# Another order for the front of an adaLN, H3 and SwiGLU kernel: its operations, buffers and loads, and which of two engines makes some additions

## The chip, the cores and the metric

One core of a Trainium2 chip runs the whole program. The time is device microseconds of one execution; three executions of the kernel before gave 583.09, 584.99 and 586.24 us, median 584.99.

The core has four compute engines with an instruction stream each: TensorE (PE in the profile, with its weight loads as PEld), VectorE (DVE), ScalarE (ACT) and GpSimd (POOL). SyncE (SP) issues the transfers between HBM and the on-chip memory SBUF. Every engine takes its instructions strictly in the order in which the program lists them for it, and waits on semaphores for what others have to deliver.

## The reference

All tensors are float32; 2048 tokens, 512 channels, 1792 hidden units.

```python
def _A_ref(q, k, v, shift_k, ssm_k, ssm_D):
    k_shift = sum over t < 4 of k[s - 3 + t] * shift_k[:, 3 - t]   # causal, per channel
    kv = k_shift * v
    y = causal convolution of kv with ssm_k (2048 taps, per channel, by FFT)
    return q * (y + kv * ssm_D)

def _B_ref(x, w_gate, w_up, w_down):
    return (_silu(x @ w_gate) * (x @ w_up)) @ w_down

x = A_q
mod = (_silu(c) @ w_mod).reshape(c.shape[0], 6, 1, -1)
sa, ca, ga, sb, cb, gb = (mod[:, 0], mod[:, 1], mod[:, 2], mod[:, 3], mod[:, 4], mod[:, 5])
h = _layernorm(x, axis=-1) * (1 + ca) + sa
x = x + ga * _A_ref(h, A_k, A_v, A_shift_k, A_ssm_k, A_ssm_D)
h = _layernorm(x, axis=-1) * (1 + cb) + sb
x = x + gb * _B_ref(h, B_w_gate, B_w_up, B_w_down)
return x
```

(`_A_ref` is abridged here to what it computes; the rest is the reference's own text.)

## The kernel before, in words

The program has two parts. The **front** computes everything up to the normalised input of the feed-forward block; the **feed-forward part** behind it is a steady stream of matmuls (tiles `a`, `b`, `c`, `d`, `g`, `dn`, `dq` in the profile).

The front treats the 512 channels as four blocks of 128, numbered 0 to 3, and the 2048 tokens as four tiles of 512, also 0 to 3. For one channel block it

- loads k, v and the long filter (`load_k`, `load_v`, `load_ssm`; tiles `kt`, `vt`, `ss`; 1 MiB each, some in halves or quarters), and four quarters of a transform table (`load_e`, tile `er`);
- forms the short convolution in tile `u`: `tap0` is a product by one column, `tap` a product and addition on VectorE over the whole block, and `tap2` the same split into a product on ScalarE (tile `tap`) and an addition on GpSimd;
- multiplies by v in four quarters (`times_v`, in place in `vt`), on VectorE or GpSimd;
- adds the skip weight to the first row of the filter (`skip`, one row of 128 numbers in `ss`);
- transposes the product (`x_turn`, TensorE, tile `kvt`, copied by ScalarE), and takes the first transform stage of product and filter (`x_first`, `kx_first`, `k_first`, `xk_first`: TensorE into tile `s`, copied by ScalarE to `X`, `K`, `kt` or `xk`);
- swaps rows and columns in 32x32 squares, either on VectorE (`swap_x`, STREAM_TRANSPOSE, four pieces of 128x1024 for a block) or on TensorE (`k_turn`, `xk_turn`);
- for each of eight halves of blocks `n`: takes the second stage (`x2`, tile `px`, copied by ScalarE to `xs`), sums two of its parts (`x_sum`, tile `xs` from two `xs`), multiplies with the filter's spectrum (`prod`, three VectorE products `xs<-pk,xs`), and transforms back (`inv`, tile `iv`, copied by ScalarE to `X`);
- sends the block's result to HBM and back in another layout (`put`, `get`; block 2's filter spectrum makes such a trip too, `put_k`, `get_k`), except for block 3, which VectorE transposes a second time;
- takes the last stage for a token tile (`y_pe`, tile `y`, with the inverse tables `ei` from `load_einv`, `load_einv2`).

Beside it, token tile by token tile, q is loaded (`load_x`, tile `x`), its row statistics are taken (`do_stats`, `do_aggr`; tiles `bnq`, `mva`, `rsa`), the normalised rows are formed by ScalarE (`gate_n`, tile `s`), and the modulation is multiplied in and added (`gate_m`, `gate_a`, two halves each, `s<-s,bcs`). The modulation comes from the loads of `w_mod` (`mod_load`, tile `wm`), a matmul group (`mod_rows`, tile `pb`), and a trip through HBM that spreads its rows (`mod_out`, `mod_in`, tile `bcs`). Then `y_gate` multiplies y by `s`, `add_c` adds the result to `x` with statistics of the new rows (`bnb`), `do_norm2a` closes those statistics (`mvb`, `rsb`), and `norm2b`, `norm_t`, `norm_s`, `op_hi` and `op_lo` make the first operands of the feed-forward part: normalised rows `n`, transposed `nt`, modulated `hraw`, and a pair of a rounded and a remaining part, `op`. `gu_pe` (tile `g`) is its first matmul group.

What sets the order: there is no scheduler at run time. The whole front is one list of 516 calls from line 1121 on, written in the order that is wanted, and each engine gets its instructions in that order. A function marked `@parts` is called several times, and each call does its next part: usually first the matmuls, then the copy out of PSUM. So the position of a call sets when an engine may take the work, and also what stands behind it in the same engine's queue. SP's transfers are issued in the list's order too, and a transfer that has to wait (for a buffer that is still read, or for the transfer that had the same completion semaphore) holds up all behind it.

Which buffer an operation gets is written out as well. `HOMES` (line 32) holds, for each kind of buffer, one digit per allocation in the list's order: `e8` the 8 KiB tiles per partition (k, v, u, filters, x), `b16` the 16 KiB ones (spectra, modulation weights), `r4` and `k2` smaller ones, `xs` the sums, `ps` the PSUM banks. An operation that gets a buffer waits until its earlier user's readers are done.

The engine of some additions is an argument of the call, with a default: `times_v`, `skip` and `op_lo` go to VectorE unless `pool` is given; `x_sum`, `gate_m` and `gate_a` go to GpSimd unless `dve` is given.

Of the kernel before, what the change touches and what calls it, by code (L numbers as in the profile page):

```python
# [33 lines left out]
        "1045324542111032544"  # L34
    ),
    "e8": (
        "630215745627041562756263424634623634642623634"
    ),
    "r4": (
        "4021342012243012403124023130432143213242304130243102413204123401243012340123240104010401"  # L40
    ),
    "k2": (
        "110212021020102010201020102010201201201201201201200112"
    ),
    "xs": (
        "10101010"
    ),
# [31 lines left out]
def adaln_h3_swiglu(ctx, tc, q, kT, vT, shk, ssm, dskip, wgu, wdn, c, wmod, e_fwd, e_inv, w_c, out, out_t):  # L79
# [1053 lines left out]
    tap(0, 3, 0)  # L1133
    tap0(0, act, 1)
    tap(0, 1, 1)
    k_first(0, 3)
    k_first(0, 2)
    k_first(0, 3)
    load_ssm(2)
    load_v(0, 1)  # L1140
    load_e(1)
    kx_first(2, 2)
    load_v(0, 2)
    tap(0, 2, 1)
# [36 lines left out]
    k_turn(0, 1)
    load_v(1)
    times_v(1, 0, pool)
    load_c()
    x_first(0, 0)
    x_first(0, 2)
    times_v(1, 1, pool)
    x_first(0, 1)
    load_ssm(1)
    swap_x(2)  # L1190
    times_v(1, 2, pool)
    k_turn(0, 0)
    load_k(2)
    load_wc()
    k_turn(0, 1)
    k_turn(0, 2)
    k_turn(0, 3)
    tap0(2, dve)
    k_turn(0, 2)
    k_turn(0, 3)  # L1200
    times_v(1, 3, pool)
    swap_x(3)
    k_first(1, 1)
    kx_first(2, 0)
# [24 lines left out]
    x_sum(1)
    tap(2, 2)  # L1230
    do_stats(2, 0)
    k_first(1, 0)
    x_first(1, 0)
    x_first(1, 1)
    x_first(1, 2)
    x_first(1, 2)
    x_first(1, 3)
    x_first(1, 1)
    k_turn(1, 2)
    k_turn(1, 2)  # L1240
    prod(1, 1)
    x_first(1, 3)
    prod(1, 0)
    tap2(2, 3, 0)
    swap_x(0)
    tap2(2, 3, 0)
    swap_x(1)
    x2(0, 2)
    prod(1, 2)
    x2(0, 2)  # L1250
    load_k(3)
    prod(1, 1)
    do_stats(3, 1)
    prod(1, 0)
    prod(1, 2)
    x2(0, 1)
    x2(0, 1)
    tap2(2, 3, 1)
    prod(0, 1)
    prod(0, 0)  # L1260
    tap2(2, 3, 1)
    times_v(2, 0, pool)
    silu_c()
    x_sum(0, dve)
    times_v(2, 2, pool)
    prod(0, 1)
# [36 lines left out]
    silu_c()
    skip(3, pool)
    tap2(3, 3, 1)
    do_aggr(3)
    do_aggr(3)
    xk_first(2, 1)
    load_x(0)
    xk_first(2, 1)  # L1310
    xk_first(2, 2)
    tap2(3, 2, 0)
    xk_first(2, 2)
    xk_first(2, 3)
# [12 lines left out]
    do_stats(2, 2)
    tap2(3, 2, 0)
    do_aggr(2)
    do_aggr(2)  # L1330
    xk_turn(2, 2)
    load_x(1)
    swap_x(6)
    tap2(3, 3, 0)
    xk_turn(2, 1)
    xk_turn(2, 1)
    x2(3, 2)
    x2(3, 2)
    load_v(3)
    x2(3, 1)  # L1340
    x2(3, 1)
    swap_x(4)
    times_v(3, 0, pool)
    x2(2, 1)
    x2(2, 1)
    do_aggr(2)
    prod(3, 0)
    times_v(3, 1, pool)
    x_sum(3, dve)
    prod(3, 0)  # L1350
    prod(3, 1)
    x2(2, 2)
    prod(3, 1)
    prod(3, 2)
    prod(3, 2)
    do_aggr(3)
    x2(2, 2)
    do_stats(0, 1)
    mod_out()
    put(0)  # L1360
    xk_turn(2, 3)
    xk_turn(2, 3)
    do_aggr(0)
    do_stats(1, 3)
    gate_n(2, 0)
    gate_n(3, 1)
    x_turn(3, 0)
    x_turn(3, 0)
    times_v(3, 3)
    inv(3)  # L1370
    gate_n(2, 1)
    prod(2, 1)
    x_sum(2, dve)
    times_v(3, 2, pool)
    x2(5, 1)
    inv(3)
    prod(2, 0)
    inv(3)
    do_aggr(0)
    prod(2, 1)  # L1380
# [442 lines left out]
```

## Time and profile before

| | |
|---|---|
| three executions | 583.09, 584.99, 586.24 us; median 584.99 |
| the profiled execution | 586.58 us, of which the span is 584.8 |
| TensorE's granted clock over the span | 0.997 |
| HBM read and written | 74.66 MB and 38.29 MB, 193 GB/s over the span |

The profile is of one execution. Times in it are microseconds from the span's start. In a row of single instructions the columns are start, duration, engine, line of the kernel, operation, tile written and tiles read, shape and count, and in brackets the idle time of the engine before it with what ended it. All instructions carry line 63, that of the helper that records them, so they are told apart by their tiles. In a row of a stretch, the columns are its bounds and width, then the busy time of each engine with the number of instructions, the clock granted to TensorE, the busy share of the 16 DMA engines, and GB/s. A row of a wait has who waited for whom, microseconds in total, times, and the longest. A row of a group has the busy time and the mean nanoseconds of one, then the idle time before them and what ended it.

### The profile page before, as it was taken

What the parts mean: (1) busy time and instruction counts of PE and PEld (TensorE: products, weight loads), DVE (VectorE), ACT (ScalarE), POOL (GpSimd) and SP (SyncE); (2) the same over time, 40 slices, a digit from 0 to 9 for tenths busy, and PEclk for the clock granted to TensorE, in tenths of its full rate; (3) what the DMA queues carried; (4) which work ended last, traced back from release to release, by engine and by line L of the source; (5) the groups of instructions that cost most, each with busy time, mean ns of one, the idle gap of its engine ahead of it and who ended that gap; (6) DMA issues with size and microseconds to landing.
All of it is one profiled execution on the core that took longest, in us unless ns stands there. A gap on an engine that the chain in (4) does not pass through costs nothing.

```text
span 584.8 us, 9918 instructions
## 1 busy us (share of the span) xinstructions
PE 565.1 (97%) x3938; PEld 442.5 (76%) x3938; DVE 461.3 (79%) x617; ACT 295.0 (50%) x442; POOL 345.9 (59%) x259
## 2 busy tenths in 40 slices
PE   4999899999899999999999999999999999999997
PEld 3984634655778888888888888888888888888885
DVE  6899778998999877877778868865577777777775
ACT  3898958783664454337354435435433333333330
POOL 0167654848035696674948794376283837374991
PEclk9999989999999999999999999999999999999999
DMA  8898998989010297191836480075343434343403
GB/s 304 349 410 340 267 319 239 346 286 365 2 73 27 116 366 282 59 351 58 299 128 209 182 307 27 3 268 199 127 162 127 161 127 161 127 161 127 162 2 143
DMA packets 41625, 113.60 MB, mean 194 GB/s; under 512 B 3157, under 2 KB 19685, under 8 KB 36074
## 3 DMA queue, kind: packets, MB, share of 16 engines
q1 hardware_dynamic: 41578, 112.96, 53.5%
q8 instruction: 31, 0.51, 0.4%
q14 instruction: 16, 0.13, 0.1%
HBM read 74.66 MB, written 38.29 MB: 193 GB/s over the span
## 4 chain that ended last, share of the span: by engine, by line
PE 69%; ACT 2%; DVE 1%; issue 1%; POOL 1%; ACTq 0%
PE dn L63 14%; PE b L63 12%; PE a L63 12%; PE c L63 12%; PE dq L63 10%; PE d L63 6%; PE g L63 3%; PE nt L63 1%; ACT n L63 1%; ACT hraw L63 1%; POOL wd L63 0%; POOL rsb L63 0%; DVE x L63 0%; DVE op L63 0%; ACT wd L63 0%
## 5 line engine op out<-in xcount | busy, mean ns | idle before, releaser
L63 PE MATMUL dn<-wd,acts 128*128 128x512 f32 x336 | 83.2, 391 | 0.1
L63 PE MATMUL b<-op,wsum 128*128 128x512 f32 x312 | 79.3, 390 | 0.0
L63 POOL TENSOR_TENSOR wa<-ws,wa 128x512 fp32r<-128x512 f32 (+1 forms) x28 | 36.2, 1314 | 64.8 <-ACT wa L63 64.8
L63 PEld LDWEIGHTS dn<-wd,acts 128*128 128x128 f32 x336 | 62.9, 188 | 13.8 <-DVE acts L63 0.5
L63 PEld LDWEIGHTS b<-op,wsum 128*128 128x128 f32 x312 | 58.5, 188 | 12.4 <-ACT p L63 0.3
L63 PE MATMUL a<-op,wa 128*128 128x512 f32 x228 | 58.1, 390 | 0.0
L63 PEld LDWEIGHTS a<-op,wa 128*128 128x128 f32 x228 | 42.7, 188 | 8.8
L63 POOL TENSOR_TENSOR acts<-sg,acts 128x512 fp32r<-128x512 f32 x16 | 23.2, 1464 | 41.6 <-ACT acts L63 41.6
L63 DVE TENSOR_TENSOR x<-x,dn 128x512 f32<-128x512 f32 x56 | 36.9, 678 | 10.9 <-PE dn L63 10.8
L63 ACT ACTIVATE sg<-sg 128x512 f32<-128x512 f32 x20 | 12.7, 633 | 65.0 <-DVE sg L63 65.0
L63 POOL TENSOR_TENSOR s<-s,bcs 128x1024 f32<-128x1024 f32 x14 | 34.3, 2476 | 12.1 <-DVE bcs L63 7.2
L63 PE MATMUL c<-op,wa 128*128 128x512 f32 x156 | 39.6, 389 | 0.0
L63 PE MATMUL c<-op,wsum 128*128 128x512 f32 x156 | 39.6, 389 | 0.0
L63 PE MATMUL d<-op,wsum 128*128 128x512 f32 x156 | 39.6, 389 | 0.0
L63 DVE STREAM_TRANSPOSE X<-X 128x1024 f32<-128x1024 f32 x16 | 35.8, 2293 | 1.1 <-ACT X L63 1.1
L63 POOL TENSOR_TENSOR wsum<-sr,wsum 128x1024 fp32r<-128x1024 f32 x14 | 35.6, 2539 | 0.0
L63 PEld LDWEIGHTS c<-op,wa 128*128 128x128 f32 x156 | 29.3, 188 | 6.1
L63 PEld LDWEIGHTS c<-op,wsum 128*128 128x128 f32 x156 | 29.3, 188 | 6.1
L63 PEld LDWEIGHTS d<-op,wsum 128*128 128x128 f32 x156 | 29.3, 188 | 6.1
L63 DVE TENSOR_TENSOR acc<-acc,dq 128x512 f32<-128x512 f32 x40 | 26.8, 684 | 6.8 <-PE dq L63 6.8
L63 ACT COPY p<-a 128x512 f32<-128x512 f32 x26 | 15.4, 591 | 33.0 <-PE a L63 33.0
L63 DVE TENSOR_TENSOR xs<-pk,xs 128x1024 f32<-128x1024 f32 x24 | 28.1, 1216 | 3.2 <-PE pk L63 2.9
(178 smaller groups left out, 1334.3 us busy)
## 6 DMA issues: line engine op xcount, KB each, us to landing
kept<-wsum SPq DMA_DIRECT2D x12, 1024.0 KB, 7.8
wsum<-kept SPq DMA_DIRECT2D x12, 1024.0 KB, 6.5
kept<-wa SPq DMA_DIRECT2D x12, 768.0 KB, 7.7
wa<-kept SPq DMA_DIRECT2D x12, 768.0 KB, 4.2
ws<-in_wgu SPq DMA_DIRECT2D x16, 512.0 KB, 5.2
wm<-in_wmod SPq DMA_DIRECT2D x6, 1024.0 KB, 9.2
x<-in_q SPq DMA_DIRECT2D x4, 1024.0 KB, 14.3
away<-X SPq DMA_DIRECT2D x2, 2048.0 KB, 13.6
```

The lines of the kernel that those rows point to most:

```text
L63: return lambda *a, **k: self.tc.keep_in_program_order(f(*a, **k))
```

## The change

The list of 516 calls of the front is written in another order, and all six digit strings of `HOMES` are other ones. The list contains the same operations; fifteen of its calls name another engine for an addition or product:

```diff
-times_v(0, 3)   times_v(0, 0)
+times_v(0, 3, pool)   times_v(0, 0, pool)
-times_v(1, 2, pool)
+times_v(1, 2)
-skip(0, pool)   skip(3, pool)
+skip(0)   skip(3)
-x_sum(1)   x_sum(0, dve)   x_sum(2, dve)
+x_sum(1, dve)   x_sum(0)   x_sum(2)
-gate_m(2, 0, dve)   gate_m(0, 1, dve)
+gate_m(2, 0)   gate_m(0, 1)
-gate_m(0, 0)   gate_m(3, 1)   gate_m(3, 0)   gate_a(3, 1)
+gate_m(0, 0, dve)   gate_m(3, 1, dve)   gate_m(3, 0, dve)   gate_a(3, 1, dve)
-op_lo("B21")
+op_lo("B21", pool)
```

(Each pair of lines collects calls that stand apart in the list.) Of the buffer table and of the list itself, the first lines:

```diff
     "b16": (
-        "1045324542111032544"
+        "1053245245111035244"
     ),
...
     load_k(0, 0)
+    load_e(1)
     load_shk()
-    load_e(2)
-    load_ssm(0, 2)
-    load_k(0, 1)
-    k_first(0, 2)
-    load_ssm(0, 3)
-    load_e(3)
     tap0(0, dve, 0)
     tap(0, 1, 0)
     tap(0, 2, 0)
     tap(0, 3, 0)
+    load_e(0)
+    load_e(3)
+    load_k(0, 1)
     tap0(0, act, 1)
```

Three places show what the new order does to the engines.

The first is SP's queue at the start of the program, before (`kt` is a k block, `er` the transform table, `ss` a filter, `vt` a v block; 128x512 is 0.25 MiB, 128x1024 0.5 MiB, 128x2048 1 MiB; `kt_161` is the second k block):

```order
L63 DMA kt_88<-in_kT 128x1024
L63 DMA shk_sb<-in_shk 128x4x4
L63 DMA er<-in_e_fwd 128x512
L63 DMA ss_93<-in_ssm 128x512
L63 DMA kt_88<-in_kT 128x1024
L63 DMA ss_93<-in_ssm 128x512
L63 DMA er<-in_e_fwd 128x512
L63 DMA ss_128<-in_ssm 128x2048
L63 DMA vt_130<-in_vT 128x512
L63 DMA er<-in_e_fwd 128x512
L63 DMA vt_130<-in_vT 128x512
```

Behind these follow one row of the skip weights, two more quarters of v, and `kt_161`. In the changed kernel the same queue, from its second k half on (ahead of it stand the first k half, three quarters of `er` and the short filter; the second k block is `kt_194`):

```order
L63 DMA kt_88<-in_kT 128x1024
L63 DMA bcs<-in_dskip 1x512
L63 DMA ss_106<-in_ssm 128x512
L63 DMA ss_108<-in_ssm 128x2048
L63 DMA ss_106<-in_ssm 128x512
L63 DMA vt_123<-in_vT 128x512 x2
L63 DMA er<-in_e_fwd 128x512
L63 DMA ss_106<-in_ssm 128x512
L63 DMA vt_123<-in_vT 128x512 x2
L63 DMA kt_194<-in_kT 128x2048
```

All four quarters of the table and three of the first filter now come ahead of the second k block, where three of the table and two of the filter did, and the last v quarters stand 0.5 MiB further back. In the middle of the front, the modulation weights, which stood in two pairs of 1 MiB loads in SP's queue, now stand in one group of four behind the last k block.

The second place is VectorE's queue in the middle of the front, around the gates. Before (`s<-s,bcs` is a gate's product or sum, `xs<-xs` an `x_sum`, `xs<-pk,xs` a `prod`):

```order
L63 SCALAR_TENSOR_TENSOR bcs<-bcs,ga 128x512
L63 TENSOR_TENSOR bcs<-bcs,ga 128x512
L63 TENSOR_TENSOR xs<-xs 128x1024
L63 TENSOR_TENSOR s_963<-s_963,bcs 128x1024
L63 TENSOR_TENSOR xs<-pk,xs 128x1024 x3
L63 BN_STATS bnq_961<-x_844 128x6
L63 BN_AGGR mva_1227<-bnq_961 128x2 x4
L63 TENSOR_TENSOR s_1068<-s_1068,bcs 128x1024
L63 TENSOR_TENSOR xs<-xs 128x1024
L63 STREAM_TRANSPOSE X_1094<-X_1094 128x32x32
```

And in the changed kernel:

```order
L63 TENSOR_TENSOR bcs<-bcs,ga 128x512
L63 BN_AGGR mva_1152<-bnq_770 128x2 x4
L63 TENSOR_TENSOR s_1101<-s_1101,bcs 128x1024
L63 TENSOR_TENSOR xs<-xs 128x1024
L63 SCALAR_TENSOR_TENSOR rsa_1157<-mva_1152,rsa_1157 128x4
L63 TENSOR_TENSOR s_992<-s_992,bcs 128x1024
L63 TENSOR_TENSOR xs<-pk,xs 128x1024 x2
L63 TENSOR_TENSOR xs<-xs 128x1024
L63 STREAM_TRANSPOSE X_1126<-X_1126 128x32x32
L63 TENSOR_TENSOR xs<-pk,xs 128x1024 x4
L63 STREAM_TRANSPOSE X_1126<-X_1126 128x32x32 x3
L63 TENSOR_TENSOR s_992<-s_992,bcs 128x1024 x2
```

Two gates of 128x1024 have come to VectorE, and the sums of two halves stand closer together, among other gates.

The third place is GpSimd's queue at the end of the front. Before (`s_1533` are the gates of token tile 1, `rsb` the reciprocal deviations of tiles 0 and 1, `sr` the first sums of the feed-forward weights):

```order
L63 TENSOR_TENSOR s_1533<-s_1533,bcs 128x1024 x3
L63 TENSOR_SCALAR rsb_1763<-mvb_1755 128x4
L63 TENSOR_TENSOR rsb_1763<-rsb_1763,mhalf 128x4
L63 TENSOR_SCALAR rsb_1916<-mvb_1882 128x4
L63 TENSOR_TENSOR rsb_1916<-rsb_1916,mhalf 128x4
L63 TENSOR_TENSOR sr<-ws 128x256
```

And in the changed kernel:

```order
L63 TENSOR_TENSOR s_1211<-s_1211,bcs 128x1024 x3
L63 TENSOR_SCALAR rsb_1724<-mvb_1719 128x4
L63 TENSOR_TENSOR rsb_1724<-rsb_1724,mhalf 128x4
L63 TENSOR_TENSOR op<-hraw,op 128x1024
L63 TENSOR_SCALAR rsb_1893<-mvb_1888 128x4
L63 TENSOR_TENSOR rsb_1893<-rsb_1893,mhalf 128x4
L63 TENSOR_TENSOR sr<-ws 128x256
```

The low part of the second operand, `op`, which VectorE made, stands on GpSimd between the two `rsb`. On TensorE, the number of `y` groups between the first `nt` group and the first `g` group goes from one to two.

More of the change, by code (lines that the diff above doesn't have):

```diff
@@ L1242, in adaln_h3_swiglu @@
[L1242 to L1266, printed above, removed]
+    k_turn(1, 0)
+    k_turn(1, 0)
+    tap0(3, dve)
+    do_stats(0, 3)
@@ new lines, in adaln_h3_swiglu @@
+    tap2(3, 3, 0)
+    x_turn(2, 0)
+    swap_x(5)
+    xk_first(2, 0)
+    swap_x(6)
+    do_stats(1, 3)
+    mod_rows()
+    x_turn(2, 1)
+    xk_first(2, 0)
+    xk_first(2, 1)
+    tap2(3, 3, 0)
+    times_v(3, 1, pool)
+    swap_x(4)
+    xk_first(2, 2)
+    xk_first(2, 3)
+    xk_first(2, 2)
+    xk_first(2, 1)
+    do_stats(1, 2)
+    get_k(2, 2, 3)
+    x2(3, 1)
+    xk_first(2, 3)
+    x2(3, 2)
+    prod(3, 2)
+    x2(3, 1)
+    do_stats(1, 0)
+    times_v(3, 0, pool)
+    x2(2, 1)
+    x2(3, 2)
@@ new lines, in adaln_h3_swiglu @@
+    x_sum(3, dve)
+    x2(2, 1)
+    x2(2, 2)
+    x2(2, 2)
+    prod(3, 2)
+    mod_out()
+    prod(3, 0)
+    prod(3, 1)
+    prod(3, 1)
+    xk_turn(2, 2)
+    xk_turn(2, 2)
+    do_aggr(2)
+    load_ssm(3)
+    do_stats(3, 2)
+    prod(3, 0)
+    skip(3)
+    times_v(3, 2, pool)
+    do_stats(3, 0)
+    do_stats(0, 1)
+    do_aggr(0)
+    xk_turn(2, 3)
+    xk_turn(2, 3)
+    put(0)
+    xk_turn(2, 0)
+    xk_turn(2, 0)
+    x_turn(3, 0)
+    x_turn(3, 0)
+    xk_turn(2, 1)
+    xk_turn(2, 1)
@@ L1306, in adaln_h3_swiglu @@
+    inv(3)
+    gate_n(2, 0)
+    inv(3)
+    inv(3)
+    x2(5, 1)
+    x2(5, 2)
+    x2(5, 2)
+    gate_n(2, 1)
+    do_aggr(0)
+    do_aggr(0)
+    do_stats(3, 1)
+    prod(2, 1)
+    prod(2, 0)
+    x2(5, 1)
+    do_stats(3, 3)
+    times_v(3, 3)
+    do_aggr(3)
+    x_sum(2)
+    prod(2, 1)
+    prod(2, 0)
+    prod(2, 2)
+    x_first(3, 1)
+    prod(2, 2)
+    inv(2)
+    mod_in()
+    gate_n(0, 2)
+    gate_n(0, 1)
     do_aggr(3)
     do_aggr(3)
-    xk_first(2, 1)
-    load_x(0)
-    xk_first(2, 1)
@@ L1339, in adaln_h3_swiglu @@
[L1339 to L1368, printed above, removed]
@@ L1480, in adaln_h3_swiglu @@
+    k_turn(3, 1)
+    inv(4)
+    load_w(1)
+    k_turn(3, 0)
+    w8_hi(1)
+    gate_a(0, 0)
+    k_turn(3, 2)
+    gate_a(3, 1, dve)
+    gate_a(0, 1)
+    gate_m(3, 0, dve)
+    get(1)
+    load_wd(0)
+    y_pe(0, 0, 1)
+    k_turn(3, 3)
+    x2(6, 2)
+    k_turn(3, 1)
+    put(2)
     w8_lo(1, dve)
-    put(2)
-    k_turn(3, 2)
+    y_gate(0, 0, 1)
+    k_turn(3, 3)
     wd_mul(0)
+    add_c(0, 0)
+    x2(6, 2)
     x2(6, 1)
     x2(6, 1)
-    k_turn(3, 0)
+    x_sum(6, dve)
+    x2(7, 1)
+    x2(7, 1)
```

592 lines of the change are left out of this document (272 added, 320 removed).

## The prediction

> **What bounds the kernel now.** I read the page's first line of busy times, then stretches of the span, then VectorE's waits, then single rows.
>
> ```profile
> span 584.8 us, 9918 instructions
> PE 565.1 (97%) x3938; PEld 442.5 (76%) x3938; DVE 461.3 (79%) x617; ACT 295.0 (50%) x442; POOL 345.9 (59%) x259
> ...
> core 0: us, PE busy (x) PEld busy (x) DVE busy (x) ACT busy (x) POOL busy (x), PEclk, DMA share, GB/s
> 0.00:152.00 152.00, 138.10 (x1980) 89.94 (x1982) 131.04 (x150) 109.21 (x135) 79.51 (x52) 0.99 0.91 310
> 152.00:160.00 8.00, 6.45 (x89) 5.58 (x86) 7.26 (x19) 7.01 (x10) 0.00 (x0) 1.00 0.01 3
> 160.00:585.00 425.00, 420.56 (x1874) 346.97 (x1873) 322.98 (x451) 178.76 (x298) 266.38 (x207) 1.00 0.42 156
> ...
> 159.78 8.55 PE L63 MATMUL g<-op,wg 128*128 128x512 f32 x36 [0.46 <-ACT hraw L63]
> ```
>
> The first row of stretches is the front, the last the feed-forward part. There TensorE is busy 420.56 of 425 us, its clock is 1.00, and its matmuls are the same before and after. So the end is the start of the first `g` matmul (159.78) plus 425.0 us, and a change of the front counts by what it does to that start. The program's last 1.8 us (586.58 of the profiled execution less its span of 584.8) are outside.
>
> TensorE's 138.10 busy us of the front are overlapping matmuls with short tiles, so I look for who it waits on. The chain before `g` runs backwards through op, hraw, the normalised rows n, and the small VectorE instruction that writes rsb, which needs the row statistics of the whole first token tile. I take VectorE as the spine:
>
> ```profile
> core 0: us, DVE busy (x), PEclk, DMA share, GB/s
> 0.00:21.50 21.50, 14.07 (x20) 1.00 0.83 297
> 21.50:79.00 57.50, 49.06 (x44) 0.97 1.00 352
> 79.00:152.00 73.00, 67.92 (x87) 1.00 0.85 281
> ...
> DVE bnq L63 <- DMA x<-in_q: 4.9, 2, 3.7
> DVE xs L63 <- ACT xs L63: 3.0, 2, 2.7
> DVE xs L63 <- PE pk L63: 2.9, 4, 1.2
> ...
> 151.82 0.16 DVE L63 SCALAR_TENSOR_TENSOR rsb<-mvb,rsb 128x4 f32<-128x4 f32 x1 [0.33 <-POOL rsb L63]
> ```
>
> VectorE works 131.04 of the 152 us; it idles 7.4 at the start, 8.4 in the middle, 5.1 late (row width less busy). rsb is done at 151.98, and `g` follows 7.8 us later. Only these 20.9 us of idling, the work of VectorE ahead of rsb, and the 7.8 us can change.
>
> **The change, term by term.**
>
> Term 1, the amount of work. Counting rows of VectorE's order up to rsb: two gate additions or products of 128x1024 more, two one-row skips more, one y gate, one sum xs<-xs, and one quarter of vt<-u,vt less; all else equal. Prices:
>
> ```profile
> L63 DVE TENSOR_TENSOR s<-s,bcs 128x1024 f32<-128x1024 f32 x2 | 2.4, 1203 | 0.0
> L63 DVE TENSOR_TENSOR s<-y,s 128x1024 f32<-128x1024 f32 x3 | 3.7, 1223 | 0.0
> L63 DVE TENSOR_TENSOR vt<-u,vt 128x512 f32<-128x512 f32 x5 | 3.2, 672 | 0.0
> L63 DVE TENSOR_TENSOR ss<-ss,bcs 1x128 f32<-1x128 f32 x1 | 0.3, 280 | 0.5 <-DMA bcs<-in_dskip 0.5
> ...
> 79.08 1.22 DVE L63 TENSOR_TENSOR xs<-xs 128x1024 f32<-128x1024 f32 x1 [2.73 <-ACT xs L63]
> ```
>
> 2 x 1.20 + 2 x 0.28 - 1.22 - 1.22 - 0.67 = -0.1 us. So the moves between VectorE and GpSimd balance; what counts is the order.
>
> Term 2, the early loads. The second block of k feeds VectorE's next run of taps.
>
> ```profile
> 0.00:20.00 20.00, 11.10 (x100) 10.27 (x102) 12.60 (x19) 7.86 (x10) 1.00 (x7) 1.00 0.88 316
> ...
> 18.87 1.28 DVE L63 TENSOR_SCALAR u<-kt,shk_sb 128x2048 f32<-128x2048 f32 x1 [1.05 <-DMA kt<-in_kT]
> 20.19 7.19 DVE L63 SCALAR_TENSOR_TENSOR u<-kt,shk_sb,u 128x2047 f32<-128x2047 f32 x3
> ```
>
> Before, this block is the last of 5.25 MiB in SP's queue and VectorE waits for it until 18.87. Now it is the last of 5.75 MiB: 0.52 MB more at 316 GB/s are 1.7 us, so it lands near 20.5. The two vt quarters that GpSimd takes over fall into that wait and save nothing. With 1.28, one skip of 0.28 and 7.19 the taps end at 29.3 instead of 27.4: **+1.9 us**. Ends: -1.1 if the load comes no later (two quarters saved, one skip added), +3.0 if the last v quarters (4.75 MiB instead of 4.25) come late as well.
>
> Term 3, the middle, from there to the sum xs<-xs that stands at 79.08. After it come, in the new order: one vt quarter, eight transposes, two first taps, three later taps, one earlier sum, ten row statistics, six products, four aggregates.
>
> ```profile
> 135.10 8.82 DVE L63 STREAM_TRANSPOSE X<-X 128x1024 f32<-128x1024 f32 x4 [0.94 <-ACT X L63]
> 109.09 3.46 DVE L63 TENSOR_TENSOR xs<-pk,xs 128x1024 f32<-128x1024 f32 x3
> 70.52 1.28 DVE L63 BATCH_NORM_STATS2 bnq<-x 128x6 f32<-128x512 f32 x2
> 71.68 0.40 DVE L63 BATCH_NORM_AGGREGATE mva<-bnq 128x2 f32<-128x6 f32 x4
> L63 DVE TENSOR_SCALAR u<-kt,shk_sb 128x2048 f32<-128x2048 f32 x3 | 4.7, 1556 | 1.1 <-DMA kt<-in_kT 1.1
> ```
>
> 0.67 + 8 x 2.2 + 2 x 1.56 + 3 x 2.40 + 1.22 + 10 x 0.64 + 6 x 1.15 + 0.40 = 43.5 us, so 72.8 if nothing waits. Two waits of the old middle go by the order: statistics of x (3.7) are taken first of the tiles queued earlier, and the sum behind 2.73 of ScalarE copies now has other work ahead. But a third of its kind appears: GpSimd's additions now stand beside VectorE's.
>
> ```profile
> 93.56 2.70 POOL L63 TENSOR_TENSOR s<-s,bcs 128x1024 f32<-128x1024 f32 x1 [7.20 <-DVE bcs L63]
> 93.94 3.39 DVE L63 TENSOR_TENSOR xs<-xs 128x1024 f32<-128x1024 f32 x1
> ```
>
> The sum takes 3.39 us beside GpSimd's gate, 1.22 alone: 2.2 us per collision. I put one such collision here, and 0.2 for the csb copy and gaps: **75.2**. Ends: 72.8, and 81.0 (79.08 + 1.9, all old waits stay).
>
> [...]
>
> Term 4, late. Before, 72.9 us pass from 79.08 to 151.98. The new order has more left there: two gates (2.41), one skip (0.28), one statistic (0.64), four aggregates (0.40) and one rsa (0.15, sized by rsb's row), less a y gate and a sum (2.44): **+1.4 us**. The late idle of 5.1 I keep as it is: the last modulation weights and the second inverse table can be requested only when the tile of the last block's products is free, as before. Ends: 2.5 less (half the idle gone), 6.5 more (three collisions). rsb is done at 75.2 + 72.9 + 1.4 = 149.5, **2.5 us earlier**.
>
> Term 5, from rsb to `g`. Two y gates and three add-and-statistics groups now stand ahead of the first op's low part, and a second block of y matmuls ahead of `g`; the second op's low part goes to GpSimd.
>
> ```profile
> 158.41 1.23 DVE L63 TENSOR_TENSOR op<-hraw,op 128x1024 fp32r<-128x1024 f32 x1 [0.60 <-ACT op L63]
> 157.36 1.09 PE L63 MATMUL y<-T,ei 128*64 128x128 f32 x16 [0.71 <-ACT hraw L63]
> L63 POOL TENSOR_TENSOR s<-s,bcs 128x1024 f32<-128x1024 f32 x14 | 34.3, 2476 | 12.1 <-DVE bcs L63 7.2
> ```
>
> Such an op costs 1.23 on VectorE and about 2.48 on GpSimd, an estimate from its gates of the same size: 1.25 more, of which 12 matmuls of the first half of `g` (12/36 of 8.55, 2.85 us) hide most. The second y block (about two rows like the one at 157.36, 1.9 us) fills a wait of 0.7 + 0.46. I take **+0.7**; ends 0 and 2.5.
>
> Sum: -2.5 + 0.7 = -1.8 us. Against its own time the profiled execution would be 584.8 us instead of 586.58. That execution lies 1.6 above the median of the three runs shown, 584.99, so I forecast **583.2 us**.
>
> **The rivals.**
>
> Faster: the new order leaves less idling than I kept. For it: waits for x tiles, 4.9 us, are named as DMA waits, and two v blocks, two x tiles and the last k block now stand ahead of all modulation weights. Against: the other waits of the front, 3.0 and 2.9 us in the rows above, are for ScalarE's copies and TensorE's products, which an order of transfers does not touch. No collision in term 3 and half the late idle gone: -1.8 - 2.2 - 2.5 = -6.5, 578.5; midway between this and the forecast lies 580.8, the time I give it.
>
> [...] Four gates on VectorE (before: two) stand between GpSimd's gates from about 88 to 115 us, as do two of VectorE's sums. Each that meets one costs 2.2. Three more than I counted give -1.8 + 6.5 = +4.7, 589.7; it decides from the third on, when it has eaten the 1.8 and a further 2.9. For it: the row at 93.94. Against: before has one clear case only, with two gates and two sums there.
>
> No effect: transfers set the front's pace, whatever their order.
>
> ```profile
> 20.00:40.00 20.00, 20.00 (x296) 18.13 (x295) 18.46 (x11) 19.69 (x28) 9.91 (x7) 1.00 0.96 382
> 40.00:60.00 20.00, 20.00 (x297) 11.54 (x295) 19.42 (x18) 17.98 (x20) 11.75 (x7) 1.00 0.91 359
> 60.00:80.00 20.00, 16.80 (x207) 9.68 (x213) 13.56 (x20) 15.05 (x20) 13.69 (x11) 0.91 1.09 292
> ...
> 64.42 3.64 PE L63 MATMUL pb<-wm,csb 128*32 128x512 f32 x32
> ```
>
> The queues are 0.88 to 1.09 busy until 80 us, the bytes are the same, and the four modulation loads (4 MiB) now stand in one block that TensorE must see before it starts the next spectra. By the rates of the rows, the 20.2 MiB up to them (21.2 MB) are through at 60 us, and those matmuls stood at 64.4 before, so I give 4 us of room. If the rate falls to the 310 of the whole front they come at 68 and the gain of the middle goes: 585.0. That the changed kernel is the same program in effect is excluded, since the orders differ on every engine.
>
> **How the numbers follow.** Chances: forecast 0.36 (581.5 to 585), faster 0.32 (577 to 582), collisions 0.19 (587 to 592), transfers 0.13 (584 to 587). Half a per cent, 2.9 us, is about what a measurement of this kernel tells from no change: the bounds are 582.1 and 587.9. Faster: 0.31 of the second case and a quarter of the first, 0.40. Slower: 0.18 of the third and 0.02 of the last, 0.20. The rest, 0.40, is no change. The range leaves out a tenth on each side: 577.5 (the faster case with little left to gain) to 589.0 (inside the collisions). The forecast's own range is 581.5 to 585.
>
> **What would show it.** Right: the second run of taps starts near 20.5; the sum xs<-xs (VectorE's second such sum) near 75; rsb near 149.5; `g` near 158; 425 us after that. Wrong: sums or gates on VectorE of 2.4 us and more beside GpSimd (collisions); statistics still behind x by several us, or TensorE waiting for the modulation weights beyond 66 us (transfers); a first op's low part more than 8.5 us behind rsb (term 5); a stretch behind `g` that is not 425 us.

## The result, and the profile after

The changed kernel takes 590.44 us (median of 5 runs, 588.74 to 591.21) against 583.86 us for the kernel before (5 runs, 583.09 to 586.24): a ratio of 1.0093, 95% interval 1.0070 to 1.0116. It is slower by 6.6 us. The forecast was 583.2 with a range from 577.5 to 589.0, so it missed in sign and in range.

The page's head for the changed kernel, and then its stretches, cut at the end of rsb and at the first `g` (columns as in the prediction):

```profile
span 589.0 us, 9923 instructions
PE 565.7 (96%) x3938; PEld 439.5 (75%) x3938; DVE 471.0 (80%) x618; ACT 295.7 (50%) x442; POOL 344.9 (59%) x258
```

```profile
0.00:156.15 156.15, 136.92 (x1946) 85.34 (x1948) 140.95 (x151) 109.60 (x135) 75.69 (x50) 1.00 0.88 302
156.15:164.39 8.24, 7.96 (x123) 7.21 (x119) 8.14 (x20) 7.23 (x10) 0.00 (x0) 1.00 0.20 67
164.39:589.00 424.61, 420.79 (x1876) 346.92 (x1874) 321.89 (x450) 178.84 (x298) 269.24 (x208) 1.00 0.42 155
```

Behind `g` nothing moved (424.6 us, before 425.0); everything is in the front, up to rsb. VectorE's busy time ahead of rsb rose from 131.0 to 141.0 us, and its idle time fell from 20.9 to 15.2. Its stretches in the changed kernel (busy time, count, clock, DMA share), and three of its rows:

```profile
0.00:22.15 22.15, 12.58 (x18) 1.00 0.91 331
22.15:76.55 54.40, 52.81 (x41) 1.00 0.95 337
76.55:156.15 79.60, 75.56 (x94) 1.00 0.83 270
```

```profile
20.76 1.29 DVE L63 TENSOR_SCALAR u<-kt,shk_sb 128x2048 f32<-128x2048 f32 x1 [0.21 <-DMA kt<-in_kT]
76.55 1.50 DVE L63 TENSOR_TENSOR xs<-xs 128x1024 f32<-128x1024 f32 x1 [0.87 <-ACT xs L63]
155.99 0.16 DVE L63 SCALAR_TENSOR_TENSOR rsb<-mvb,rsb 128x4 f32<-128x4 f32 x1 [0.33 <-POOL rsb L63]
```

| point (us) | before | forecast | after |
|---|---|---|---|
| second k block, later taps start | 20.19 | 22.1 | 22.17 |
| sum xs<-xs of n=3 starts | 79.08 | 75.2 | 76.55 |
| rsb done | 151.98 | 149.5 | 156.15 |
| first `g` | 159.78 | 158.0 | 164.39 |

(22.1 is the forecast 20.5 of the first tap plus 1.28 for it and 0.28 for the skip.) The forecast is right as far as the sum, to 1.4 us, and fails between it and rsb: 79.6 us pass there, where 72.9 + 1.4 = 74.3 were forecast.

**What TensorE did meanwhile** shows in its rows around that sum. First the kernel before, then the changed kernel; a row is a start, a duration, the matmuls' operands and count, and in brackets the idle time ahead and what ended it.

```profile
68.89 2.96 PE L63 MATMUL kt<-ident,xk 128*128 128x128 f32 x24 [0.82 <-ACT xk L63]
74.23 4.49 PE L63 MATMUL px<-X,wc 64*32 64x512 f32 x48 [2.38 <-DVE X L63]
78.52 1.91 PE L63 MATMUL pk<-T,wc 64*32 64x512 f32 x32
...
84.12 2.83 PE L63 MATMUL iv<-xs,wc 32*64 32x512 f32 x48
```

```profile
72.42 1.95 PE L63 MATMUL px<-X,wc 64*32 64x512 f32 x32
74.17 1.06 PE L63 MATMUL pk<-T,wc 64*32 64x512 f32 x16
75.02 1.92 PE L63 MATMUL px<-X,wc 64*32 64x512 f32 x32
76.74 1.92 PE L63 MATMUL pk<-T,wc 64*32 64x512 f32 x32
78.59 3.16 PE L63 MATMUL kt<-ident,xk 128*128 128x128 f32 x24
...
83.45 1.16 PE L63 MATMUL kt<-ident,xk 128*128 128x128 f32 x8 [0.74 <-DVE xs L63]
84.54 2.83 PE L63 MATMUL iv<-xs,wc 32*64 32x512 f32 x48
```

The new order puts px and pk of n=3 ahead of 24 transposes kt<-ident,xk; the old one has them behind. So the sum, which waits for px, came 2.5 us earlier in the profile, and 3.2 us of TensorE's work went from ahead of it to behind it. At the inverse `iv` of n=3 both kernels have issued the same matmuls in the same numbers (grouped by form, all eleven counts agree), and there the changed kernel is 0.4 us *later*. The 2.5 us were never a gain. By the pk products of n=6 it is 3.1 us later (128.44 against 125.33), at `g` 4.6.

Idle time of TensorE from 0 to 120 us (row width less busy) in these two profiles:

```profile
0.00:120.00 120.00, 107.59 (x1521) 0.99 0.95 321
```

```profile
0.00:120.00 120.00, 104.55 (x1488) 1.00 0.93 317
```

Before (the first row) it idles 12.4 us, after 15.4: 3 us more, and 2.6 of them lie in the first 20 us (11.5 against 8.9).

### The profile page after: what moved, and what is told of

The parts are those of the page before. It is cut to its first block, busy times and chain, and to the rows that moved or that the text cites. A ratio compares the mean times of both kernels' runs of the same rounds, so it can differ in the third digit from the quotient of the medians.

```text
span 589.0 us, 9923 instructions
## 1 busy us (share of the span) xinstructions
PE 565.7 (96%) x3938; PEld 439.5 (75%) x3938; DVE 471.0 (80%) x618; ACT 295.7 (50%) x442; POOL 344.9 (59%) x258
## 4 chain that ended last, share of the span: by engine, by line
PE 70%; DVE 1%; ACT 1%; POOL 1%; issue 0%; ACTq 0%
PE dn L63 14%; PE b L63 12%; PE a L63 12%; PE c L63 12%; PE dq L63 10%; PE d L63 6%; PE g L63 3%; PE nt L63 1%; PE y L63 1%; POOL wd L63 0%; POOL rsb L63 0%; ACT hraw L63 0%; ACT n L63 0%; DVE x L63 0%; DVE hraw L63 0%; DVE op L63 0%
## 5 line engine op out<-in xcount | busy, mean ns | idle before, releaser
L63 PEld LDWEIGHTS b<-op,wsum 128*128 128x128 f32 x312 | 58.5, 188 | 12.4 <-ACT p L63 0.3
L63 DVE TENSOR_TENSOR x<-x,dn 128x512 f32<-128x512 f32 x56 | 37.0, 678 | 11.5 <-PE dn L63 11.4
L63 DVE STREAM_TRANSPOSE X<-X 128x1024 f32<-128x1024 f32 x16 | 37.2, 2380 | 0.9 <-ACT X L63 0.9
L63 PEld LDWEIGHTS d<-op,wsum 128*128 128x128 f32 x156 | 29.3, 188 | 6.1
L63 PEld LDWEIGHTS c<-op,wa 128*128 128x128 f32 x156 | 29.3, 188 | 6.1
L63 PEld LDWEIGHTS c<-op,wsum 128*128 128x128 f32 x156 | 29.3, 188 | 6.1
L63 POOL TENSOR_TENSOR s<-s,bcs 128x1024 f32<-128x1024 f32 x12 | 29.8, 2506 | 3.9 <-ACT s L63 3.8
L63 ACT COPY p<-a 128x512 f32<-128x512 f32 x26 | 15.4, 591 | 32.4 <-PE a L63 32.4
L63 POOL TENSOR_TENSOR vt<-u,vt 128x512 f32<-128x512 f32 x12 | 16.3, 1393 | 25.8 <-DVE u L63 15.6
```

The lines of the kernel that those rows point to most:

```text
L63: return lambda *a, **k: self.tc.keep_in_program_order(f(*a, **k))
```

## The experiments

The times are medians; a ratio is to executions of the kernel before on the same chip, measured beside each experiment, with medians between 584.1 and 585.0. The changed kernel's own ratio is 1.0093 (1.0070 to 1.0116). It was not measured again beside the experiments, so a difference from its 590.44 us counts only where the two intervals lie apart: they do for e3, e8 and e9.

**Is it the meetings of VectorE and GpSimd?** The prediction's slower rival gave 589.7 for that, close to the result. It had gates and sums in mind; behind 76 us these do not meet GpSimd as it said (the four gates take 1.2 us each, the four sums 1.21 to 1.82). But three of four rsa steps, 128x4 elements that need 0.15 us, take 1.22, 2.33 and 2.35 us beside GpSimd, and VectorE waits 2.4 us more for GpSimd's half of rsa. The third of these steps, and the gate of GpSimd beside it:

```profile
99.71 2.35 DVE L63 SCALAR_TENSOR_TENSOR rsa<-mva,rsa 128x4 f32<-128x4 f32 x1 [0.92 <-POOL rsa L63]
99.65 2.38 POOL L63 TENSOR_TENSOR s<-s,bcs 128x1024 f32<-128x1024 f32 x1
```

e1 moves the last rsa step to GpSimd; e2 does the same in the kernel before.

```diff
         pool.tensor_tensor(rs[:, 0, :], rs[:, 0, :], mhalf, op=ALU.pow)
+        if name[0] == "a":
+            pool.tensor_tensor(rs[:, 1, :], m, rs[:, 0, :], op=ALU.mult)
+            pool.tensor_scalar(rs[:, 1, :], rs[:, 1, :], -1.0, None, op0=ALU.mult)
         yield
-        dve.scalar_tensor_tensor(rs[:, 1, :], m, -1.0, rs[:, 0, :], op0=ALU.mult, op1=ALU.mult)
+        if name[0] != "a":
+            dve.scalar_tensor_tensor(rs[:, 1, :], m, -1.0, rs[:, 0, :], op0=ALU.mult, op1=ALU.mult)
```

> The changed kernel with the last step of the first norms' statistics (rsa, 128x4, the product of mean and reciprocal deviation) on GpSimd right behind the power, instead of on VectorE; nothing else. Theory (VectorE pays for meeting GpSimd at this step): VectorE loses 2.4 us of waits for rsa and about 5.4 us in which three of these 0.15 us instructions took 1.22, 2.33 and 2.35 us; the time falls from 590.4 by 4 to 8 us, to 582.5 to 586.5, and rsb comes 4 to 8 us before 156.15. Rival (the list's order costs it elsewhere, and these waits would only move to the next instruction of VectorE): 589.5 to 591.

> The same edit in the kernel before, as a control. There the four rsa steps of VectorE took 0.15 us each and waited for nothing. Theory of the meeting point: no change, 583 to 585. Rival (the step is dear by itself wherever it stands): 2 us less or more.

e1: 590.44 us (ratio 1.0097, 1.0070 to 1.0125); e2: 585.29 (1.0012, 0.9994 to 1.0030). No change in either. VectorE's waits between 75 and 130 us, after first, then e1 (total, times, longest):

```profile
DVE rsa L63 <- POOL rsa L63: 2.4, 2, 1.5
DVE X L63 <- ACT X L63: 0.9, 1, 0.9
DVE xs L63 <- ACT xs L63: 0.9, 1, 0.9
```

```profile
DVE xs L63 <- PE pk L63: 6.1, 3, 3.6
DVE xs L63 <- ACT xs L63: 2.6, 1, 2.6
DVE X L63 <- ACT X L63: 0.9, 1, 0.9
```

The meetings of rsa went, and VectorE stands 6.1 us for TensorE's products instead. What had looked like a VectorE with 75.6 busy us in 79.6 was one that had slack behind TensorE and spent it beside GpSimd: the waiting inside those three steps (5.90 us together, where each needs 0.15) is counted as busy. So the rival's number was near, but its gates and sums did not collide, and the collisions that this test took out were not the cause. One of another kind is left, late: add_c(0,1) (e8, e10).

**Is it the choice of engines?** e3 is the new order with the old 15 choices, e4 the old order with the new ones.

```diff
...
-    x_sum(1, dve)
+    x_sum(1)
...
-    x_sum(0)
+    x_sum(0, dve)
...
-    gate_m(0, 0, dve)
+    gate_m(0, 0)
...
```

> The changed order, loads and buffers, with the fifteen engine choices of the kernel before. Theory (the meeting of rsa with GpSimd's queue comes from the order): the rsa step still waits and still is blocked, 588.5 to 593. Rival (the engine choices are the loss): back to 583 to 586.

> The kernel before with the fifteen new engine choices alone. Theory (order): within 2 us of before, 582 to 586, since its four rsa steps stay where they are. Rival (engine choices): 587 or more.

e3: 593.15 us (1.0151, 1.0122 to 1.0181); e4: 601.26 (1.0296, 1.0264 to 1.0327). Each order wants its own choices: in the new one the old choices cost 2.7 us more than the new, and in the old one the new choices cost 16.7 us, where e4's first theory allowed 2. So putting the old choices back does not win the loss back; with the old choices the new order is some 8.5 us slower than the old order. With the new choices it is the old order that is slower, by 10.8 us, so order and choices have no prices of their own. "Order" here is the list with its transfers and its buffer table; apart from e5's opening no run parts these.

**TensorE or VectorE?** e6 issues the pk matmuls of n=2 twice in the kernel before, e15 in the changed one; e7 adds four VectorE operations to the kernel before.

```diff
-    def pair(t, n, w, r, name):
+    def pair(t, n, w, r, name, times=1):
...
-        for g in range(4):
+        for g in [*range(4)] * times:
...
-        ps = pair(K, n, WK, r, "pk")
+        ps = pair(K, n, WK, r, "pk", 2 if n == 2 else 1)
```

```diff
     x_sum(2, dve)
+    for _ in range(4):
+        dve.tensor_scalar(R[2, 0], R[2, 0], 1.0, None, op0=ALU.mult)
```

> The kernel before, with the pk matmuls of the third products (n=2, three products) issued twice into the same banks: 48 more matmul rows, 2.8 us by 5.6 us for 96, on TensorE between 90 and 100 us, nothing else. Theory T: the time rises by 2 to 2.8 us, to 586 to 587 from 584. Theory V: TensorE has slack behind VectorE, 0 to +0.8 us.

> The kernel before, with four one-input VectorE operations of 128x1024 added behind the sum xs<-xs at 93.94 (each multiplies that sum by 1; by the row of 1.29 us for 128x2048 some 0.65 us each, 2.6 us in all). Theory V: the time rises by 2 to 2.6 us. Theory T: VectorE waits 2.5 us for TensorE and ScalarE between 86 and 106 us, which takes it up: 0 to +1 us. Both may bind, so that both this and the TensorE probe cost: then neither alone is the pace.

> The changed kernel with the pk matmuls of n=2 issued twice, as e6 did with the kernel before: 48 more rows, 2.8 us on TensorE near 90 us. Theory T: +2 to +2.8 us, 592.5 to 593.2. Theory V (here VectorE, with its meetings, is the pace and TensorE has slack behind it): 0 to +0.8.

e6: 587.13 us (1.0056, 1.0034 to 1.0078), 2.6 above the kernel before for 2.8 us of work. e7: 585.45 (1.0022, 1.0002 to 1.0042), 0.9 above for the 2.88 us that the four took; they stand at 84.25 in its trace, behind the sum of n=2, not behind the one at 93.94 that the expectation names. e15: 592.85 (1.0128, 1.0093 to 1.0163), 2.4 above the changed kernel, or 2.0 by the ratios, whose intervals overlap. Near 90 us TensorE sets the pace in the kernel before, and VectorE has some 2 us of slack there; in the changed kernel e1 and e15 say the same, e15 less surely.

**TensorE's idle pieces.** e5 gives the changed kernel the old opening (the first loads are quarters of ss and er, with the transforms that need them); the table of homes follows the order of allocation. e14 adds two more: the quarter ss(0,0) and skip(0) ahead of the second k block, and e1's rsa step.

```diff
     load_k(0, 0)
-    load_e(1)
     load_shk()
+    load_e(2)
+    load_ssm(0, 2)
+    load_k(0, 1)
+    load_ssm(0, 3)
+    load_e(3)
     tap0(0, dve, 0)
...
```

> The changed kernel with the loads and the first transforms of the kernel before in the first 20 us (first the 0.25 MB quarters of ss with their share of er, then the whole ss block); from the second k block on nothing is changed, and the buffers keep their tenants. Theory T (TensorE sets the pace from about 14 us to the sixth products near 130 us, and what it idles before 20 us shifts all that follows): the changed kernel's TensorE idles 11.5 us of the first 20 and the kernel before 8.9, so idle falls to 8.9-9.5, rsb comes 2 to 2.8 us earlier (153.4 to 154.2 instead of 156.15) and the run takes 587.5 to 588.5 instead of 590.4. Theory V (VectorE is the only bound, and its meetings with GpSimd are the loss): no change, 590 to 591. Theory O (the loss is the order of the late part, behind 120 us): no change.

> The changed kernel with three of TensorE's idle pieces taken out: the opening of the kernel before (as in e5: idle of the first 20 us 11.5 to 9.5), the quarter ss(0,0) and skip(0) ahead of the load and first tap of the second k block (0.6 us <-DVE ss), and the last rsa step on GpSimd (as in e1: 0.74 us <-DVE xs at 83.45). Theory T: TensorE idles 2.5 to 3.3 us less until 130 us, and the time falls by as much, to 587.2 to 588. Theory V: 590 to 591.

e5: 590.94 us (1.0114, 1.0096 to 1.0133), no gain. Its TensorE idled 2.0 us less in the first 20 us, and 0.96 us more in the next 20, behind a skip and a GpSimd product. e14: 589.18 (1.0072, 1.0048 to 1.0096), 1.3 below the changed kernel, where 2.4 to 3.2 were expected; the intervals overlap, so even the 1.3 is not clear of noise. These are the profiles' numbers (start of the pk matmuls of n=6, and of `g`):

| us | idle of TensorE, 0 to 120 | pk of n=6 | `g` |
|---|---|---|---|
| before | 12.4 | 125.33 | 159.78 |
| after | 15.4 | 128.44 | 164.39 |
| e1 | 13.7 | 126.42 | 163.22 |
| e5 | 14.1 | 127.59 | 164.41 |
| e14 | 11.0 | 125.58 | 162.38 |

Less idle brings the products forward, by 2.9 us for 4.4 us in e14. But with e14's products within 0.3 us of where the kernel before has them, its `g` is 2.6 us later: behind 125 us the new order has a loss of its own. In the changed kernel it begins with an addition on VectorE, add_c(0,1), which stands ahead of the last products, and TensorE's inverse of n=7 waits for those:

```profile
135.05 2.79 DVE L63 TENSOR_TENSOR x<-x,s 128x512 f32<-128x512 f32 x1
139.92 3.93 PE L63 MATMUL iv<-xs,wc 32*64 32x512 f32 x48 [1.94 <-DVE xs L63]
```

The kernel before has no wait there. e1, e5 and e14 have the same wait (TensorE idles 2.06, 2.02 and 2.07 us from 130 to 140 us, in the changed kernel 2.02), and in their profiled executions the granted clock behind it is lower: 0.84 in e1 and 0.83 in e5 from 140 to 150 us, 0.92 and 0.91 in e14 from 130 to 140 and from 140 to 150; in the changed kernel's profile it is 1.00 in both. So 1.7 of e14's 2.6 us (10 x 0.08 + 10 x 0.09) are this loss of clock. Without it, from the pk of n=6 to `g`, the changed kernel takes 36.0 us against 34.5.

e13 takes out one idle piece of the kernel before: three swaps on VectorE, for which px waits 2.38 us, stood behind statistics that wait for a load of x. e17 adds e2's rsa step.

```diff
     swap_x(7)
+    swap_x(5)
+    swap_x(6)
+    swap_x(4)
     do_stats(0, 2)
...
-    swap_x(5)
...
-    swap_x(6)
...
-    swap_x(4)
```

> The kernel before with one change in VectorE's order: the transposes swap_x(5), (6) and (4) stand directly behind swap_x(7), ahead of the two statistics of block 0 of x, on whose load VectorE stands idle there (3.70 us <-DMA x<-in_q at 67.24). Theory T (TensorE's idle time is what counts): TensorE no longer waits 2.38 us for DVE X ahead of px of n=3, which the changed kernel's order had won too, and the time falls by 1.8 to 2.4 us, to 582 to 582.8. Theory V (VectorE's busy time and its meetings with GpSimd set the pace): VectorE's own idle falls as well, so it must fall; if the time stays within 0.7 us both are wrong about this place.

> The kernel before with the swaps of e13 ahead and the last rsa step on GpSimd as in e1 and e2. In e13 a new wait had come where the old one went: VectorE waited 1.48 us for GpSimd's rsa and took 1.95 us for a 128x4 step (it needs 0.15), and TensorE idled 0.60, 1.25 and 0.49 us behind it. Theory T: these go, 1.2 to 2.3 us less than e13's 583.7, 581.5 to 582.5. Theory V as e1 and e2 had it (moving that step costs and brings nothing): 583.5 to 584.

e13: 583.72 us, ratio 0.9964 (0.9941 to 0.9987), 1.3 below the kernel before by the medians, ahead of both kernels, and short of the 582 to 582.8 expected; e17: 583.41, ratio 0.9986 (0.9971 to 1.0002). Part of e13's gain seems to be a loss of clock that it is spared with the wait (last section): all 12 of its executions had a mean clock of 0.999 or 1.000, and against the 17 of the kernel before beside them that had that too, median 584.19, it is 0.5 lower; e17 is 0.7 lower in the same way (584.13). In e13's trace the wait ahead of px is gone, and new ones stand behind it:

```profile
60.72 8.81 DVE L63 STREAM_TRANSPOSE X<-X 128x1024 f32<-128x1024 f32 x4
73.63 1.95 DVE L63 SCALAR_TENSOR_TENSOR rsa<-mva,rsa 128x4 f32<-128x4 f32 x1 [1.48 <-POOL rsa L63]
...
71.27 2.81 PE L63 MATMUL px<-X,wc 64*32 64x512 f32 x48
78.10 1.16 PE L63 MATMUL kt<-ident,xk 128*128 128x128 f32 x8 [0.60 <-DVE xs L63]
80.52 0.75 PE L63 MATMUL kvt<-ident,vt 128*128 128x128 f32 x4 [1.25 <-DVE rsa L63]
```

e17 was to win those too and did not show it: its expectation of 581.5 to 582.5 is missed, and its interval overlaps that of e13.

**The place of the transposes.** e9 puts 16 of the 24 transposes ahead of px of n=3 again, with the last copy of xk (`xk_first(2, 3)`) that they need, and deals their banks anew; e16 is the same kernel, run once for its profile.

```diff
+    xk_first(2, 3)
+    xk_turn(2, 2)
+    xk_turn(2, 2)
+    xk_turn(2, 3)
     x2(3, 1)
-    xk_first(2, 3)
+    xk_turn(2, 3)
...
-    xk_turn(2, 2)
-    xk_turn(2, 2)
...
-    xk_turn(2, 3)
-    xk_turn(2, 3)
...
```

> The changed kernel, but on TensorE 16 of the transposes kt<-ident,xk of block 2 (2.0 us; 24 took 3.16) stand ahead of px and pk of n=3, as in the kernel before, not behind them; their banks are dealt anew, nothing else. Theory A (the sum xs<-xs of n=3 is a point from which the rest follows at a fixed distance, as the prediction had it): that sum comes 2 us later (78.5 instead of 76.55), and so do rsb and the time: 592 to 593. Theory T (TensorE is dense from 14 to 130 us, so what counts is the work and the idle time on it and not when one row of it comes): the sum comes 2 us later, the inverse of n=3 starts where it did (84.5), rsb and the time stay within 0.7 us of 156.15 and 590.4.

> The kernel of e9 once more, for its profile: it took 2.8 us more than the changed kernel where theory T had allowed 0.7. Theory T now: ahead of the 16 transposes TensorE waits 2 to 3 us for the last copies of xk on ScalarE (the kernel before waited 0.82 us for them there and 2.38 for the swaps), and the inverse of n=3 starts that much behind 84.5; the work itself costs nothing by its place. Theory A: TensorE waits for nothing new, and the end moves with the sum.

e9: 593.25 us (1.0155, 1.0127 to 1.0184), 2.8 above the changed kernel; e16 took 595.51. Theory A's number came; theory T, as e9 states it, allowed 0.7 and missed. Two TensorE rows of e16, and then TensorE's stretch from 74 to 78 us (busy time, count, clock, DMA share, GB/s):

```profile
73.47 3.04 PE L63 MATMUL kt<-ident,xk 128*128 128x128 f32 x16 [2.24 <-ACT xk L63]
87.14 2.84 PE L63 MATMUL iv<-xs,wc 32*64 32x512 f32 x48 [0.26 <-ACT x L63]
```

```profile
74.00:78.00 4.00, 4.00 (x38) 0.57 1.08 347
```

There is a new wait of 2.24 us, and the inverse of n=3 starts 2.6 us behind 84.54. Both are as theory T was restated for e16, ahead of its trace (a wait of 2 to 3 us, and the inverse that much later); theory A had no new wait. The four us at a granted clock of 0.57 behind the wait cost 4 x 0.43 = 1.7 in e16; three of e9's executions had a mean clock of 1.000 and took 592.86 to 593.25 us, so e9's 2.8 us do not need it. Within the changed kernel its own order of this place is the better one: it hides that wait.

**The late part.** e8 moves the y gate of tile 0 ahead of two gates and a weight cast, and add_c(0,1) behind the last products; e10 moves add_c(0,1) next to add_c(0,0), where GpSimd waits.

```diff
-    gate_a(3, 1, dve)
...
-    gate_m(3, 0, dve)
...
-    w8_lo(1, dve)
     y_gate(0, 0, 1)
+    gate_a(3, 1, dve)
+    gate_m(3, 0, dve)
+    w8_lo(1, dve)
...
-    add_c(0, 1)
...
     prod(7, 2)
+    add_c(0, 1)
```

```diff
     add_c(0, 0)
+    add_c(0, 1)
...
-    add_c(0, 1)
```

> The changed kernel with the late part reordered on VectorE: y_gate(0,0,1) stands ahead of two gates and of the low part of wg, and add_c(0,1) behind the last two products of n=7. Theory O: px of block 3 starts up to 0.75 us earlier, the last products end 3.6 us earlier, the inverse of n=7 no longer waits 1.9 us for them, and the time falls by 2 to 3.6 us, to 587 to 588.5. Theory T and theory V: VectorE is dense from 117 to 152 us, so the order of its work there moves single rows and not the last transposes: 0 to -0.8 us.

> The changed kernel with add_c(0,1) directly behind add_c(0,0), near 129 us, where GpSimd waits for ScalarE, and not among the last products, where GpSimd runs its gates. Theory L (the 2.79 us that this 128x512 addition takes there are a meeting with a gate; alone it takes 0.69): it takes 0.69 us, VectorE, dense from 117 to 152 us, has 2.1 us less to do, the last transposes, rsb and the time come 1.5 to 2.1 us earlier, 588.3 to 589. Theory T: the sixth products start 1.6 us later, TensorE's inverses behind them too, and the end stays: within 0.7 us of 590.4.

e8: 592.16 us (1.0137, 1.0119 to 1.0155), slower by 1.7, where its theory had 2 to 3.6 less; e10: 589.97 (1.0102, 1.0074 to 1.0130), no change. e10 shows why moving this meeting away alone did not help; the addition takes 0.68 there, and the next sum meets GpSimd in its place:

```profile
128.20 0.68 DVE L63 TENSOR_TENSOR x<-x,s 128x512 f32<-128x512 f32 x1
128.91 0.87 DVE L63 BATCH_NORM_STATS2 bnb<-x 128x6 f32<-128x128 f32 x4
129.69 2.65 DVE L63 TENSOR_TENSOR xs<-xs 128x1024 f32<-128x1024 f32 x1
```

TensorE's wait moved with it: the inverse of n=7 no longer waits, but the last pk matmuls wait for VectorE's `xs` instead, 2.65 us in e10, and 3.07 in e8, where the sum takes 2.50.

**The price of a meeting.** e11 and e12 put four 128x4 operations among the last swaps of the kernel before, beside six gates of GpSimd, with two inputs and with one.

```diff
+        dve.tensor_tensor(junk[:, 8:12], junk[:, 0:4], junk[:, 4:8], op=ALU.add)
...
+    tiny()
     swap_x(12)
...
```

> The kernel before with four VectorE additions of 128x4 (two inputs in SBUF, a tile of their own, no one waits for them), one ahead of each of the last four transposes of X between 135 and 144 us, while GpSimd runs six gates back to back from 130.18 to 144.38. Theory L (a VectorE operation with two SBUF inputs waits until GpSimd's running operation ends, however small it is): the four take 3 to 9 us together instead of 4 x 0.15, and the time rises by 2 to 7 us. Theory N (there is no such meeting; the rows of 2.3 us have another cause): 0.6 us together, no change of the time.

> The control of the run before: the same four 128x4 operations in the same places, with one SBUF input each (times 1). Theory L and theory N: 0.1 to 0.15 us each, the time within 0.7 us of the kernel before.

e11: 588.08 us (1.0064, 1.0034 to 1.0095); e12: 588.71 (1.0071, 1.0044 to 1.0097). The control cost the same. e12's rows, and the six gates of GpSimd beside them:

```profile
131.02 0.82 DVE L63 TENSOR_SCALAR junk<-junk 128x4 f32<-128x4 f32 x1
134.23 2.29 DVE L63 TENSOR_SCALAR junk<-junk 128x4 f32<-128x4 f32 x1
138.66 0.22 DVE L63 TENSOR_SCALAR junk<-junk 128x4 f32<-128x4 f32 x1
140.98 0.36 DVE L63 TENSOR_SCALAR junk<-junk 128x4 f32<-128x4 f32 x1
...
127.13 14.18 POOL L63 TENSOR_TENSOR s<-s,bcs 128x1024 f32<-128x1024 f32 x6
```

Spread evenly, a gate takes 14.18/6 = 2.36 us, and four of the six end at 131.86, 136.58, 138.95 and 141.31; the four operations end at 131.84, 136.52, 138.88 and 141.34. Each ends with the gate that is running, though it has only 128x4 elements. Together they take 3.69 us (e11: 3.60), and the time rises by 3.4 us in e11 and 4.0 in e12. Part of the rise is the clock: seven of e11's ten executions and six of e12's seven had a mean clock between 0.988 and 0.997; the other three of e11 have a median of 586.77, 2.6 above the kernel before at such a clock (584.19). In this stretch, unlike near 90 us, VectorE's time is on the path.

## Why the prediction was wrong

**The spine** was mistaken: "I take VectorE as the spine". Its own quoted rows had TensorE busy 20.00 of 20.00 us twice, from 20 to 60 us, but it set TensorE's 138.10 busy us aside as overlapping matmuls with short tiles. e6 against e7, with e1 and e15, shows that TensorE bounds the stretch near 90 us; from 131 to 141 us VectorE's time counts, as e11 and e12 show in the kernel before.

**Term 1** counted 0.1 us less VectorE work; its busy time rose by 9.9. The count of instructions was right; the rise is their lengthening beside GpSimd. The three rsa steps make 5.5 us of it, and e1 took them out without effect; add_c(0,1) makes 2.1, late.

**Term 2** was right: the second k block's first tap starts at 20.76 (forecast 20.5), the taps end at 29.27 (29.3).

**Term 3** was right in its number to 1.4 us, down to the one collision it put there (the earlier sum takes 2.75 us beside GpSimd), and wrong in its meaning. "75.2" is the time of one row that the new order had put ahead of 3.2 us of TensorE's work. That row's old time, 79.08, also held a wait of 2.38 us that statistics behind a late load had caused (e13), and px at a lower clock behind it (0.57 from 74 to 78 us, 1.00 from 71 to 75 in e13): 48 matmuls took 4.49 us, 2.81 in e13.

**Term 4** is the step that failed: "Before, 72.9 us pass from 79.08 to 151.98", carried over with 1.4 us more work. It took 79.6, 6.7 us more than before and 5.3 more than forecast. Of the 6.7, 2.9 lie ahead of the inverse of n=3, because 3.2 us of transposes now stand behind the sum: a distance between two VectorE rows was carried over although TensorE's work inside it had grown. Another 2.7 lie between that inverse and the pk of n=6. There TensorE idles 1.2 us instead of 0.3 (0.75 of it for VectorE's y gate), and the same matmuls keep it busy 42.7 us instead of 40.9, for a reason that no run shows. The last 1.1 lie between that and rsb, with the wait of 1.94 us for products behind add_c(0,1), 2.79 us where it needs 0.69. e8 and e10 moved that wait and did not win it back, so which order would do so stays open.

**Term 5** forecast +0.7 from rsb to `g`; it was +0.4 (8.24 against 7.80), and the 425 us behind it held.

**The base**: the profiled execution of the kernel before took 586.58 us, 2.7 above the median of its later runs; the sum took off 1.6. The old profile holds a loss of clock of 1.7 us (last section) that most executions of that kernel, by their mean clock, do not have. The changed kernel's profile stands only 0.3 above its median. So of the 6.6 us between the medians 4.2 are seen between the two profiles (4.6 at `g`, less 0.4 behind it), and the other 2.4 come from where the two profiled executions stand among their kernel's runs: the old one was long for its kernel.

**The rivals**: the faster one counted VectorE's idling, which did fall, from 20.9 to 15.2 us, while the time rose; it failed with the spine. The collisions of gates and sums did not come; those of rsa did, and their removal brought nothing (e1). That the slower rival's 589.7 lies near 590.44 is luck. Transfers as the pace of the whole front were not seen either (the modulation matmuls start at 64.50, before at 64.42); but the first ss block, which TensorE starts with, landed at 11.14 us instead of 6.65, and TensorE idled 2.6 us more in the first 20.

What the runs establish is which engine bounds two stretches, and that the old engine choices do not undo the loss. They do not add up to 6.6 us: the most that an edit of the changed kernel took back is e14's 1.3, and that is not clear of noise.

## What to carry to other kernels

A row may serve as a milestone only if the change leaves the same work ahead of it on every tight engine; count the instructions on each side of it before a later stretch is carried over. An engine that shows no idle time for 40 us is a bound until an added or removed microsecond on it shows otherwise, and the busy time of VectorE beside GpSimd is an upper bound of its work (2.35 us for a step that takes 0.15 elsewhere in the same trace). Where a wait was taken out of a dense stretch, the next one stood close behind (e1, e10, e13): e13 took out 2.4 us of waiting and kept 1.3 by the medians, 0.5 at equal clock, and e14 at most 1.3 of 4.4.

## What the runs showed of the hardware

**A wait of TensorE can cost twice.** In the kernel before, TensorE's clock in the four us behind the 2.38 us wait was:

```profile
74.00:78.00 4.00, 3.77 (x40) 0.57 1.06 368
```

That is 4 x 0.43 = 1.7 us on top of the wait. Microsecond by microsecond from 74 the clock is 0.64, 0.50, 0.50 and 0.66. e16 shows the same behind 2.24 us (0.57), and e1, e5 and e14 late, behind 2.02 to 2.07 us of idle time (0.83 to 0.92 over ten us); in e7 a wait of 2.48 us at the same place, and in the changed kernel the wait of 1.94, cost no clock (1.00 behind both). What tells the two cases apart no run shows. It seems to be one part of why executions of one kernel differ: of the 94 executions of the kernel before that were measured beside the experiments, 81 had a mean clock of 0.999 or 1.000 and a median of 584.41 us, and 12 had 0.996 or 0.997 and 587.13 (one more, at 0.991, took 593.30). e13 and e17, which take out the wait of 2.38 us, had 0.999 or 1.000 in all 24. The difference of 2.7 us is more than the 1.7 of one such loss, and what makes the rest is not shown.

**One input was enough for a meeting.** In e12 a multiplication of 128x4 by a constant took 2.29 us and ended at 136.52, with GpSimd's gate (136.58), as the addition of two tiles in the same place in e11 took 2.27 and ended at 138.39, with a gate at 138.46, while the swaps beside e12's gates took 2.17 to 2.35 us.
